# A fused attention and long-convolution kernel: the first quarter of x emptied in four chunks by two engines, the queries' bank emptied in one operation, the filter copies given other planned durations

## The chip, the cores and the metric

One core of a Trainium2 chip. It has a matrix engine (PE in the profile, its weight loads PEld), a vector engine (DVE), an activation engine (ACT), a general engine (POOL) and an engine that only issues transfers (SP). PE writes its results to eight banks of PSUM, each 128 partitions by 512 fp32 numbers; DVE and ACT empty them into SBUF. The metric is the device time of one execution in microseconds, median of several; lower is better.

## The reference

The kernel computes two things and puts them side by side: a multi-head attention block (2048 tokens, width 512, 32 heads of 16) and a long convolution with gates on the same shape. Cut to its core:

```python
def _A_ref(x, wqkv, wo):                      # x: 2048 x 512
    q, k, v = split_heads(x @ wqkv)           # 32 heads of 16
    scores = einsum("bhqd,bhkd->bhqk", q, k) * 16 ** -0.5
    p = softmax(scores)
    return merge_heads(einsum("bhqk,bhkd->bhqd", p, v)) @ wo

def _B_ref(q, k, v, shift_k, ssm_k, ssm_D):   # each of q, k, v: 2048 x 512
    kv = causal_conv4(k, shift_k) * v
    y = causal_long_conv(kv, ssm_k)           # 2048 taps per channel, by FFT
    return q * (y + kv * ssm_D)

out = concatenate([a, b], axis=-1)
```

## The kernel before

**Attention.** The scores are made in blocks of 128 keys by 512 queries for one head; there are 2048 such blocks (4 quarters of queries, 8 groups of 4 heads, 16 key tiles). Blocks are worked off in 695 steps, called T in the code, of two or three blocks each. In a step PE makes the blocks' scores (line L690) into two or three neighbouring PSUM banks, and ACT takes the exponential of the whole step in one ACTIVATE (L697) into the tile PT. In 260 of the steps the last block goes to DVE instead: L713 takes it out of its bank, and six short passes over pairs or fours of such blocks (L746 to L753) make the exponential there. PE then multiplies by the values (L787). The steps alternate between banks 0 to 2 and 3 to 5; bank 6 collects the products with the values, and bank 7, BGB in the code, serves everything else ("background").

**What is made ahead.** Queries QT, keys KTo and values VAF come out of projections of x (L396, L403, L441), each 128 x 512 in a bank that DVE empties (L419, L433, L452). The queries of a bank belong to two groups of heads; they are emptied twice, each time multiplied by another column of the mask MSK (evac_q, two TENSOR_SCALARs of 128 x 512). x arrives in quarters of 512 tokens. The last three are turned by the transfer itself; the first is turned on PE (turn_x, L375, 16 transposes), and its two halves are emptied by one ACTIVATE (L382) and one COPY (L384), 128 x 1024 each. The first query projection needs both halves.

**The convolution.** The taps are laid out for it by 16 filter copies, each of which is two COPYs of 128 x 1440 and 128 x 1380 (L502) and a short one (L508, from KZ0, which POOL makes out of the taps at L492 and L493). They are written to memory and come back in shifted pieces (WR). They read the taps that the transfers into QT, EI and JNK bring. The convolution itself is 8192 small matmuls (L944), whose moving operand is read in runs of 4 numbers.

**What sets the order.** The program is written by a planner in the file itself. It keeps a clock for each engine, adds an assumed duration for each operation, and decides step by step which piece of background, which pass on DVE and which filler goes where. The assumed durations set the order of instructions and nothing else. Each engine then works its list in order and waits on semaphores alone. On DVE the planner subtracts DVE_OVER (0.084 us) from what an operation is given. KZ_US is the assumed duration of half a filter copy; such a half is put in place when DVE's clock leaves room for it, and at the latest four steps after its turn. keep_share adds filler matmuls (L1114) where the planner finds PE too little used. At the start, `warm` runs 12 matmuls on zeros (L536). At the end, wait_busy runs filler matmuls (L1298) until the last transposed result of DVE (L828) is due, which the last output projection (L868) needs.

## Time and profile before

| | us |
|---|---|
| median of 3 runs | 833.1 (832.81 to 834.8) |
| the profiled execution, its own time | 833.18 |
| its span, first to last instruction | 831.4 |
| ACT busy | 813.6 (98%) |
| DVE busy | 788.7 (95%) |
| PE busy | 728.8 (88%) |

A group of instructions is read like this: line, engine, operation, what is written and read with its shape, how many, then busy time, mean duration of one in ns, and idle time of the engine just before them with the operation that ended it. The mean duration is longer than the distance from one instruction to the next where instructions of one engine overlap. In a timeline the columns are start, length, engine, line, and a count where neighbours are merged; in square brackets stands the idle time before and what ended it. The chain of waits goes back from the last instruction to whatever released it each time; its rows are start and length.

### The profile page before, as it was taken

The numbers are of one execution on the slowest core, as the hardware profiler recorded it, in microseconds if no ns is written. First come the engines' busy times: TensorE is split into PE (matmuls) and PEld (weight loads), VectorE is DVE, ScalarE is ACT, GpSimd is POOL, SyncE is SP. The second block draws the span as 40 slices with busy tenths as digits, with TensorE's granted clock in tenths as the row PEclk, the third lists the DMA queues.
The fourth block names the chain that finished last, engine by engine and source line by source line (L and its number), as shares of the span: only waits on it lengthen the run. The fifth ranks groups of instructions, "written<-read, shape, count | busy, mean of one in ns | idle before, by whom it ended". The sixth has DMA issues, their size and how long they took to land.

```text
span 831.4 us, 30085 instructions
## 1 busy us (share of the span) xinstructions
PE 728.8 (88%) x13456; PEld 322.7 (39%) x13456; DVE 788.7 (95%) x1423; ACT 813.6 (98%) x701; POOL 15.7 (2%) x35
## 2 busy tenths in 40 slices
PE   8888999988888889888889898988888888888997
PEld 3332334344434433334434444334443444434322
DVE  3799999999999999999999999999999999999995
ACT  6999999999999999999999999999999999999997
POOL 3000000000000001000000000000000000000000
PEclk9999999999999999999999999999999999999999
DMA  9977502058767776867775889567777988858200
GB/s 241 294 287 248 158 2 76 1 137 267 239 200 228 233 226 199 223 192 228 229 222 166 278 238 275 183 199 220 260 218 261 265 284 267 286 160 258 74 1 26
DMA packets 123856, 167.31 MB, mean 201 GB/s; under 512 B 50384, under 2 KB 55504, under 8 KB 123472
## 3 DMA queue, kind: packets, MB, share of 16 engines
q1 hardware_dynamic: 120752, 162.77, 63.1%
q8 instruction: 106, 1.74, 0.8%
q10 hardware_dynamic: 2400, 1.05, 0.6%
q0 software_dynamic: 576, 1.57, 0.5%
q14 instruction: 22, 0.18, 0.1%
HBM read 143.14 MB, written 16.52 MB: 192 GB/s over the span
## 4 chain that ended last, share of the span: by engine, by line
ACT 82%; DVE 10%; PE 4%; SPq 2%; DMA 1%; issue 1%; POOL 0%; DVEq 0%
ACT PT L697 82%; SPq L278 2%; DVE WR L502 1%; DVE EI L713 1%; PE PS L690 1%; DVE EI L753 1%; DMA JNK<-in_B_ssm_D_dram 1%; PE PS L787 1%; DVE EA L749 1%; DVE QT L419 1%; DVE KTo L433 1%; PE PS L465 1%; DVE EA L748 0%; DVE xT L746 0%; DVE EA L746 0%
## 5 line engine op out<-in xcount | busy, mean ns | idle before, releaser
L697 ACT ACTIVATE PT<-PS 128x1024 bf16<-128x1024 f32 (+1 forms) x695 | 809.7, 1417 | 5.5 <-PE PS L690 4.9
L690 PE MATMUL PS<-QT,KTo 32*128 32x512 bf16 x2048 | 272.5, 385 | 83.6 <-ACT PT L697 61.4
L787 PE MATMUL PS<-PT,VAF 128*32 128x512 bf16 x1788 | 226.3, 391 | 0.9
L944 PE MATMUL PS<-WR,KV 128*8 128x64 bf16 (+15 forms) x8192 | 183.6, 214 | 2.5 <-issue 2.0
L713 DVE TENSOR_SCALAR EI<-PS 128x512 int32<-128x512 f32 x260 | 173.9, 682 | 1.5 <-PE PS L690 1.1
L944 PEld LDWEIGHTS PS<-WR,KV 128*18 128x18 bf16 (+15 forms) x8192 | 150.1, 119 | 47.4 <-issue 24.2
L690 PEld LDWEIGHTS PS<-QT,KTo 32*128 32x128 bf16 x2048 | 70.9, 91 | 235.3 <-ACT PT L697 213.0
L753 DVE SCALAR_TENSOR_TENSOR EI<-EI,EA 128x1024 int32<-128x1024 int32 (+1 forms) x146 | 156.5, 1098 | 0.0
L787 PEld LDWEIGHTS PS<-PT,VAF 128*32 128x32 bf16 x1788 | 53.6, 93 | 92.2 <-issue 86.6
L1114 PE MATMUL PS<-ZR,IDN 128*128 128x512 bf16 (+3 forms) x299 | 84.0, 333 | 0.0
L749 DVE TENSOR_TENSOR EA<-EA,xT 128x1024 f16<-128x1024 f16 x114 | 75.2, 683 | 0.0
L746 DVE TENSOR_SCALAR xT<-EI 128x1024 f16<-128x1024 uint16 x114 | 74.0, 684 | 1.3
L752 DVE TENSOR_TENSOR EA<-EA,xT 128x1024 bf16<-128x1024 f16 x114 | 75.0, 682 | 0.0
L787 PE MATMUL PS<-EI,VAF 128*32 128x512 bf16 x260 | 56.3, 410 | 1.3 <-DVE STG L835 0.6
L750 DVE TENSOR_SCALAR xT<-xT 128x1024 f16<-128x1024 f16 x114 | 45.1, 418 | 0.0
L748 DVE TENSOR_SCALAR EA<-xT 128x1024 f16<-128x1024 f16 x114 | 44.0, 420 | 0.0
L1114 PEld LDWEIGHTS PS<-ZR,IDN 128*128 128x128 bf16 x299 | 23.2, 97 | 32.3 <-issue 23.0
L787 PEld LDWEIGHTS PS<-EI,VAF 128*32 128x32 bf16 x260 | 13.1, 93 | 32.6 <-issue 14.2
L835 DVE STREAM_TRANSPOSE STG<-PS 128x512 f32<-128x512 f32 x31 | 22.0, 711 | 3.4 <-PE PS L787 3.3
L419 DVE TENSOR_SCALAR QT<-PS,MSK 128x512 bf16<-128x512 f32 x32 | 22.6, 741 | 1.2 <-PE PS L396 1.2
L403 PE MATMUL PS<-xT,WKV 128*128 128x512 bf16 x60 | 19.4, 386 | 3.8 <-DVE VAF L452 1.3
L396 PE MATMUL PS<-xT,WQ 128*128 128x512 bf16 x64 | 20.1, 385 | 2.1 <-ACT xT L382 0.8
(72 smaller groups left out, 317.2 us busy)
## 6 DMA issues: line engine op xcount, KB each, us to landing
WR<-kz_scratch SPq DMA_DIRECT2D x512, 256.0 KB, 4.0
kz_scratch<-WR SPq DMA_DIRECT2D x16, 752.0 KB, 4.4
QN<-in_B_q_dram SPq DMA_DIRECT2D x16, 128.0 KB, 4.2
out_dram<-KV SPq DMA_DIRECT2D x16, 128.0 KB, 4.1
out_dram<-OUTA POOLq DMA_DIRECT2D x12, 128.0 KB, 2.9
QT<-in_B_ssm_k_dram SPq DMA_DIRECT2D x1, 1024.0 KB, 5.6
EI<-in_B_ssm_k_dram SPq DMA_DIRECT2D x1, 1024.0 KB, 8.4
STG<-in_B_v_dram SPq DMA_DIRECT2D x1, 1024.0 KB, 7.4
```

What stands on the lines that cost most here:

```text
L690: ins = e.matmul(PS[:, bank, :], lhsT=KTo[32 * s:32 * s + 32, g // 2, kt * 128:(kt + 1) * 128], rhs=QT[32 * s:32 * s + 32, qb % 2, g, :], ...
L697: h_exp[T] = act.op(lambda e: e.activation(PT[:, T % R_PT, 0:n * QB], PS[:, banks[0]:banks[0] + n, :].rearrange("p b f -> p (b f)"), ACT.E ...
L713: s.fix.append(dve.op(lambda e: e.tensor_scalar(EI[:, i, :], PS[:, bank, :], FIX_LO, FIX_ADD, ALU.max, ALU.add), [h] + old + [x for o in s ...
L746: step(2, lambda sl: lambda e: e.tensor_scalar(eb[:, sl], frac[:, sl], FS / OCT, -FS * ROOT0, ALU.mult, ALU.add), s.fix + old)
L748: step(4, lambda sl: lambda e: e.tensor_scalar(ea[:, sl], eb[:, sl], FS * (ROOT0 - ROOT1), None, ALU.add))
L749: step(2, lambda sl: lambda e: e.tensor_tensor(ea[:, sl], ea[:, sl], eb[:, sl], ALU.mult))
L750: step(4, lambda sl: lambda e: e.tensor_scalar(eb[:, sl], eb[:, sl], C1 * BITS / FS ** 3, (C0 + C1 * ROOT0) * BITS / FS ** 2, ALU.mult, AL ...
L752: step(2, lambda sl: lambda e: e.tensor_tensor(eg[:, sl], ea[:, sl], eb[:, sl], ALU.mult))
L753: step(1, lambda sl: lambda e: e.scalar_tensor_tensor(ei[:, sl], ei[:, sl], BITS / OCT, eg[:, sl], ALU.mult, ALU.add), ends=True)
L787: ins = e.matmul(PS[32 * s:32 * s + 32, pvb(qb * NG + g), :], lhsT=VAF[:, kt, h * VW:h * VW + 32], rhs=rhs, start=(order[b] == 0), stop=(o ...
L944: ins = e.matmul(PS[32 * c:32 * c + NW - 2 * n, BGB, col:col + 64], lhsT=KV[:, 2 * n:NW, 4 * qd + c], rhs=w, start=(n == 0), stop=(n == NB ...
L1114: return e.matmul(PS[:, bank, col:col + 128 * k], lhsT=IDN[:, :], rhs=ZR[:, :].rearrange("p (m d) -> p m d", m=1).broadcast_to([128, 4 * k ...
```

## The change

Four things change. The first quarter of x is turned in four groups of four transposes, each into a bank of its own, and emptied by four operations of 128 x 512, two on DVE and two on ACT in turn; the first query projection is issued in four pieces, each of which waits for its own chunk alone; 10 matmuls stand in `warm` where 12 stood, on bank 4. The queries' bank is emptied by one TENSOR_TENSOR that writes both groups (128 x 1024 out of 128 x 512 read twice, times the mask's two columns spread out); only the very first one, for group 0 of quarter 0, keeps the old pair. The planner is told 0.57 us and 0.19 us for the parts of a filter copy in place of 0.5 and 0.22. And before the last filler of the end, 32 small matmuls of VAF with itself are put in, in four kinds that differ in how the moving operand is read (runs of 4, of 2, of 1, and one whole run of 64 numbers). Nobody reads what they write.

```diff
-KZ_US = .5
+KZ_US = .57
...
-    def turn_x(sc, cp, bank, eng):
-        pbf = PS[:, bank, :].bitcast(BF16)
+    def turn_x(sc, c, bank, eng):
+        pbf = PS[:, bank, 0:256].bitcast(BF16)
...
-            for i in range(2):
-                for t in range(4):
-                    c = 2 * cp + i
-                    ins = e.transpose(pbf[:, 512 * i + 128 * t:512 * i + 128 * t + 128],
-                                      KVE[:, 4 * sc + t, 128 * c:128 * c + 128], IDN[:, :])
+            for t in range(4):
+                ins = e.transpose(pbf[:, 128 * t:128 * t + 128], KVE[:, 4 * sc + t, 128 * c:128 * c + 128], IDN[:, :])
...
-            deps += h_x[qb] + [h_wq[min(o, 1)]]
+            deps += (x or h_x[qb]) + [h_wq[min(o, 1)]]
...
+    def evac_both(qb, o, bank, h):
...
+        src = PS[:, bank, :].rearrange("p (m f) -> p m f", m=1).broadcast_to([128, 2, QB])
+        par = MSK[:, :].rearrange("p (m f) -> p m f", f=1).broadcast_to([128, 2, QB])
+        bank_free[bank] = h_q[(qb, 2 * o)] = h_q[(qb, 2 * o + 1)] = dve.op(
+            lambda e: e.tensor_tensor(QT[:, qb % 2, 2 * o:2 * o + 2, :], src, par, ALU.mult), [h, h_msk], us=1.24)
...
-        h_kzp[i] = dve.op(lambda e: e.tensor_copy(KZS[:, i % 4, :, 0, :], k0), [h_kzt[0], h_kz0] + hs, us=0.22)
+        h_kzp[i] = dve.op(lambda e: e.tensor_copy(KZS[:, i % 4, :, 0, :], k0), [h_kzt[0], h_kz0] + hs, us=0.19)
...
-    pe.op(lambda e: warm(e, 12, 0), [h_w0], us=3.5)
-    turn_x(0, 0, 0, act)
-    turn_x(0, 1, 1, dve)
-    hq = pe_unit(("q", 0, 0), 6)
+    pe.op(lambda e: warm(e, 10, 4), [h_w0], us=3.0)
+    for c in range(4):
+        turn_x(0, c, c, act if c % 2 else dve)
+    hq = None
+    for c in range(4):
+        hq = pe_unit(("q", 0, 0), 6, [c], [h_xc[c]])
...
+    def wait_busy0(bank):
...
+        def runs_of_1(e):
+            return [e.matmul(PS[32 * c:32 * c + 32, bank, 0:64], lhsT=VAF[:, n, 32 * c:32 * c + 32], rhs=va(n, [[68, 64]]),
+                             start=True, stop=True, tile_position=(0, 32 * c)) for n in range(2) for c in range(4)][-1]
...
+        for fn in (runs_of_4, runs_of_2, runs_of_1, whole_runs):
+            pe.op(fn, [h_idn, bank_free[bank]], us=0.16)
...
     for t in range(4):
+        if t == 0:
+            wait_busy0(0)
         wait_busy(when_of(h_otn[(NQB * NO - 1, 2 * (t // 2) + 2)]), 0)
```

The planner makes a new order out of this, on DVE from the passes over the first pair of blocks on. The numbers of instructions stay where they were: 695 exponentials on ACT (398 of three blocks, 297 of two), 260 blocks on DVE, 32 filter-copy halves; the fillers on L1114 go from 299 to 296. Lines after the new functions are 6 higher (L690 becomes L696, L697 L703, L713 L719, L433 L437, L868 L874).

DVE in the opening, from the seventh emptied block of keys (KTo) to the eighth, before:

```order
L433 CAST KTo<-PS 128x512
L835 STREAM_TRANSPOSE STG<-PS 128x512
L502 COPY WR<-EI 128x24x60
L813 RECIPROCAL DR<-STG 128x32
L817 TENSOR_TENSOR OB<-STG,DR 128x2x16x16
L477 TENSOR_TENSOR KV<-PS,STG 128x4x128
L502 COPY WR<-EI 128x23x60
L508 COPY WR<-KZ 128x47x4
L502 COPY WR<-EI 128x24x60
L828 STREAM_TRANSPOSE OT<-OB 128x512
L433 CAST KTo<-PS 128x512
```

The same stretch in the changed program:

```order
L437 CAST KTo<-PS 128x512
L841 STREAM_TRANSPOSE STG<-PS 128x512
L506 COPY WR<-EI 128x24x60
L819 RECIPROCAL DR<-STG 128x32
L481 TENSOR_TENSOR KV<-PS,STG 128x4x128
L506 COPY WR<-EI 128x23x60
L512 COPY WR<-KZ 128x47x4
L823 TENSOR_TENSOR OB<-STG,DR 128x2x16x16
L719 TENSOR_SCALAR EI<-PS 128x512
L506 COPY WR<-EI 128x24x60
L437 CAST KTo<-PS 128x512
```

The transpose of OB has moved behind the block of keys, and a block of scores (L719) is taken from its bank ahead of it; a second L719 has moved ahead of the seventh block in the same way. From the start to the eighth block of keys DVE's list now holds two more L719, one transpose less, and one L423 in place of one pair of L419.

PE at the end of the program, before (L787 is the last product with the values, L1298 the fillers, L868 the last output projections):

```order
L787 MATMUL PS<-PT,VAF 32x512 x2
L868 MATMUL PS<-WKV,OT 128x512
L868 MATMUL PS<-WKV,STG 128x512
L1298 MATMUL PS<-IDN 128x512 x3
L868 MATMUL PS<-WKV,STG 128x512 x2
```

And now:

```order
L793 MATMUL PS<-PT,VAF 32x512 x2
L874 MATMUL PS<-WKV,OT 128x512
L874 MATMUL PS<-WKV,STG 128x512
L1310 MATMUL PS<-VAF 32x64 x8
L1314 MATMUL PS<-VAF 32x64 x8
L1318 MATMUL PS<-VAF 32x64 x8
L1322 MATMUL PS<-VAF 32x64 x8
L1298 MATMUL PS<-IDN 128x512
L874 MATMUL PS<-WKV,STG 128x512 x2
```

Two of the three fillers have given way to the 32 small matmuls.

38 lines of the change are left out of this document (23 added, 15 removed).

## The prediction

> **What bounds the kernel now.** I read the page's first part and its costliest groups first, then the table by stages, to see which engine has no room left and where.
>
> ```profile
> PE 728.8 (88%) x13456; PEld 322.7 (39%) x13456; DVE 788.7 (95%) x1423; ACT 813.6 (98%) x701; POOL 15.7 (2%) x35
> ...
> L697 ACT ACTIVATE PT<-PS 128x1024 bf16<-128x1024 f32 (+1 forms) x695 | 809.7, 1417 | 5.5 <-PE PS L690 4.9
> ...
> 25.00:100.00 75.00, 65.00 (x546) 24.50 (x543) 71.40 (x164) 71.79 (x64) 0.39 (x4) 1.00 0.81 262
> ...
> 600.00:700.00 100.00, 86.66 (x2099) 42.03 (x2096) 97.16 (x161) 98.90 (x86) 1.08 (x2) 0.98 0.83 261
> ```
>
> In the stage rows the busy times are those of PE, PEld, DVE, ACT and POOL. ACT is the bound: even in the latest of the stages shown it is idle 1.1 us in 100, where DVE has 2.8, and 809.7 of its 813.6 us are the exponentials. The order of the changed program still holds 398 + 297 of them in the same two shapes, so these 809.7 us stay. What can move is what lies around them, which ACT's timeline shows (start, length, then the idle time before):
>
> ```profile
> 9.80 18.44 ACT L697 ACTIVATE PT<-PS 128x1536 bf16<-128x1536 f32 x16 [0.75 <-PE PS L690]
> ...
> 28.63 10.77 ACT L697 ACTIVATE PT<-PS 128x1024 bf16<-128x1024 f32 x10 [0.39 <-PE PS L690]
> ...
> 73.88 36.97 ACT L697 ACTIVATE PT<-PS 128x1024 bf16<-128x1024 f32 x31 [0.75 <-PE PS L690]
> ...
> 454.81 198.32 ACT L697 ACTIVATE PT<-PS 128x1536 bf16<-128x1536 f32 x169 [0.39 <-PE PS L690]
> 653.89 1.46 ACT L697 ACTIVATE PT<-PS 128x1536 bf16<-128x1536 f32 x1 [0.76 <-PE PS L690]
> 655.68 168.59 ACT L697 ACTIVATE PT<-PS 128x1536 bf16<-128x1536 f32 x146 [0.33 <-PE PS L690]
> ```
>
> The first exponential starts at 9.80, the last ends at 655.68 + 168.59 = 824.27. Check: 9.80 + 809.7 + (5.5 - 0.75) idle = 824.25. The end takes 831.4 - 824.27 = 7.1 us, and 833.18 - 831.4 = 1.8 us lie outside the span. After 100 us the idle time is 0.39 + 0.76 + 0.33 = 1.5 us; so 5.5 - 0.75 - 1.5 = 3.25 us lie between 28 and 100 us, where DVE is busy 71.40 of 75. Everything that the change can win is in four places: 9.80 at the start, 3.25 in the opening, 1.5 later, 7.1 at the end.
>
> **The start.** PE turns the quarter at 5.61; both halves must be out before the queries' matmuls start.
>
> ```profile
> 5.61 1.06 PE L375 MATMUL PS<-IDN,KV 128*128 128x128 bf16 x16
> ...
> 6.25 1.02 ACT L382 ACTIVATE xT<-PS 128x1024 bf16<-128x1024 bf16 x1 [1.42 <-PE PS L375]
> ...
> 7.50 1.02 PE L396 MATMUL PS<-xT,WQ 128*128 128x512 bf16 x4 [0.83 <-ACT xT L382]
> ...
> L884 ACT ACTIVATE QT<-PS 128x512 bf16<-128x512 f32 x2 | 1.2, 597 | 3.2 <-PE PS L868 3.2
> ```
>
> In chunks, ACT takes its first at 6.25 as now (eight transposes are done then) for 0.60, its second from 6.85 to 7.45 at the latest, or 0.25 us earlier if two ACTIVATEs overlap as the exponentials do (mean 1417 ns, 809.7/695 = 1165 ns apart). Three of the four matmuls are over by then; the last comes 0.23 us after its chunk, as now (7.27 to 7.50), and takes 0.39, as the single L868 at 826.31 does further down. The queries are ready at 7.8 to 8.07 in place of 8.52, so the first exponential starts 0.45 to 0.7 us earlier. The two matmuls fewer in `warm` fall into PE's wait for x, which ends with x's landing and not with them. But the gain is met again at 28 us. The chain of waits of the first 100 us runs there:
>
> ```profile
> 15.38 8.21 DMA JNK<-in_B_ssm_D_dram
> ...
> 25.60 0.61 DVE VAF L452
> ...
> 28.30 0.69 DVE KTo L433
> ```
>
> The taps land at 23.6 by SP's own sequence, which the change does not touch. DVE's first filter copy waits for them, the values' bank (L452) is queued behind it, PE's next projection behind that, and the keys come out at 28.30; the exponential of 28.63 waits for these. DVE's list is the same up to there in both programs. So ACT arrives 0.45 to 0.7 earlier and waits that much longer: I count **0**, with bounds -0.7 (all kept) and 0 (what is done earlier makes nothing later).
>
> **The opening, 28 to 100 us.** From 28.30 on the chain lies almost wholly on DVE.
>
> ```profile
> 30.91 0.60 DVE EI L713
> ...
> 76.37 0.62 DVE OT L828
> 76.99 0.57 DVE KTo L433
> ...
> 80.81 1.32 DVE QT L419 x2
> ...
> 192.11 2.28 DVE EI L753 x2
> ```
>
> Up to the eighth block of keys (76.99 here) the new list holds two more L713 (+2 x 0.60), a transpose less (-0.62), and one wide operation for a pair. The wide operation is in no trace. Bounds of its distance: 1.14, as 128 x 1024 of L753 (2.28 for two), and 1.32 as the pair; the nearest rows are products out of PSUM and with a spread fp32 operand:
>
> ```profile
> L974 DVE TENSOR_TENSOR KV<-PS,QN 128x512 bf16<-128x512 f32 x16 | 10.9, 680 | 0.6 <-PE PS L964 0.6
> ...
> L817 DVE TENSOR_TENSOR OB<-STG,DR 128x512 bf16<-128x512 f32 x15 | 10.4, 690 | 0.4
> ...
> L753 DVE SCALAR_TENSOR_TENSOR EI<-EI,EA 128x1024 int32<-128x1024 int32 x114 | 135.3, 1215 | 0.0
> ...
> L753 DVE SCALAR_TENSOR_TENSOR EI<-EI,EA 128x512 int32<-128x512 int32 x32 | 21.2, 681 | 0.0
> ```
>
> At 128 x 512 they last as long as L753 (680, 690, 681 ns), so I take L753's 1.14: -0.18. Sum on DVE: 1.20 - 0.62 - 0.18 = +0.4. Behind the two L713 are then the next keys, queries and PE's score matmuls that need them. Since ACT has two blocks less by then and catches them up later (1592 - 1182 = 410 ns each by the two exponential rows below), the worst is 0.4 + 0.82 = +1.2.
>
> ```profile
> L697 ACT ACTIVATE PT<-PS 128x1536 bf16<-128x1536 f32 x398 | 559.8, 1592 | 2.8 <-PE PS L690 2.5
> L697 ACT ACTIVATE PT<-PS 128x1024 bf16<-128x1024 f32 x297 | 301.9, 1182 | 2.8 <-PE PS L690 2.4
> ...
> 34.73 1.34 DVE L502 COPY WR<-QT 128x1440 bf16<-128x1440 bf16 x2
> 35.99 0.24 DVE L508 COPY WR<-KZ 128x188 bf16<-128x188 bf16 x1
> ```
>
> Against this stands the planner's better knowledge. Half a filter copy really takes (35.99 - 34.73)/2 = 0.63; the planner counted 0.5 - 0.084 = 0.42 and now counts 0.49: a third of the miss (0.07 of 0.21) is gone, and urgent banks are less often queued behind a copy thought shorter. If a third of the 3.25 us idle goes with it, that is -1.1. Bounds of the whole stage: -3.25 and +1.2; I take +0.4 - 1.1 = **-0.7**.
>
> **After 100 us.** Twelve of the fifteen wide operations stand here, 12 x 0.18 = 2.2 us less on DVE. ACT is busy 98.90 of 100 us there by the stage's row, which hides it: 0. Without that cover it would be up to -2.2, but the exponentials alone then set the pace, and there is nothing below them. The 1.5 us idle are the clock's:
>
> ```profile
> 448.61:452.02 3.41, 2.40 (x65) 1.29 (x56) 3.41 (x8) 3.41 (x4) 0.00 (x0) 1.00 0.88 280
> 452.02:455.43 3.41, 3.40 (x45) 0.99 (x47) 3.41 (x5) 3.02 (x4) 0.00 (x0) 0.50 0.53 173
> ...
> 650.00:653.41 3.41, 1.42 (x48) 0.77 (x35) 2.72 (x4) 3.13 (x3) 0.00 (x0) 1.00 0.58 124
> 653.41:656.82 3.41, 3.41 (x64) 1.36 (x61) 2.87 (x6) 2.60 (x2) 0.00 (x0) 0.50 0.92 254
> ...
> 652.88 0.49 PE L944 MATMUL PS<-WR,KV 128*30 128x64 bf16 x23 [1.67 <-issue]
> ```
>
> Behind a stretch with PE busy 2.40 or 1.42 of 3.41 us follows one with the granted clock at 0.50, and ACT waits in it. The second begins with 1.67 us in which PE waited for nothing shown. The Trainium skill ("TensorE: Matmul & The Clock Gate", Part 1: The HAM clock gate) has the clock fall after an idle window of about 3.4 us; the trace disagrees, since PE was busy 2.40 of 3.41 us before the first fall. By that rule a new order could not bring such a stretch, by the rows it can. Bounds: -1.5 (none) to +3.0 (three times as much); with 296 fillers for 299 I take **0**.
>
> **The end.** The last output projection waits for DVE (L828) until 826.31.
>
> ```profile
> 825.10 0.81 PE L1298 MATMUL PS<-IDN 128*128 128x512 bf16 x3
> ...
> 826.31 0.39 PE L868 MATMUL PS<-WKV,STG 128*128 128x512 bf16 x1 [0.41 <-DVE STG L828]
> ...
> 649.50 0.68 PE L944 MATMUL PS<-WR,KV 128*14 128x64 bf16 x32
> ```
>
> The 32 new matmuls have the convolution's size, 32 of which take 0.68; with one filler (0.27, a third of 0.81) they end by 825.10 + 0.95 = 826.05, before 826.31. Cost **0**; if each took twice as long, 826.73, so +0.4; with the 0.21 us of a full 512-column step for each group of four, 8 x 0.21 + 0.27 = 1.95, so +0.75 at the most. The Trainium skill ("SBUF — State Buffer", Door 1: The DMA port swizzle) says that reading slows when fewer than two numbers of a 16-byte line are used in turn, which would hit the runs of one; no row here shows it, and it stays inside these bounds.
>
> **Sum.** 833.18 + 0 - 0.7 + 0 + 0 = **832.5 us**, made against the profiled execution, which stands 0.1 us above the median of 833.1. 0.3% of it, 2.5 us, is about what a measurement of this kernel can tell from no change.
>
> **The rivals.** Faster: the opening is really opened. The start's 0.6 is kept, since the new order feeds ACT other work at 28 us, and two thirds of the 3.25 us go without the +0.4: 833.18 - 0.6 - 2.2 - half of the clock's 1.5 = 829.6. For it: DVE's own idle time there is 75 - 71.40 = 3.6 us, so DVE is not full. Against it: the landing at 23.6.
>
> Slower, by the clock: a new order, planned with the same miss about PE, leaves PE too little used in more stretches. One fall cost 0.39 us of idle time, the other 0.76 + 0.33 = 1.1; three more of the dearer kind make 833.18 + 3.3 = 836.5, and the time is slower by over 0.3% from the third on. For it: before one of the falls PE was busy 70%, not far below its 87% of a whole stage. Against it: only two falls in 212 stretches of 3.41 us between 100 and 824 us so far.
>
> Slower, by the wide operation: if DVE does not take a bank read twice at the pace of L974, and needs twice the 1.14, twelve times 1.14 = 13.7 us come on a DVE that has 2.84 idle in 100, and each holds up whatever L713 is queued behind it, whose bank PE's next scores need; if two thirds reach ACT, 833.18 + 9 = 842. Against it speak the rows of L974 and L817.
>
> Without effect on the sign: the two early L713 cost their full 1.2 and the end 0.4, so 833.18 + 1.6 = 834.8, within 0.3%.
>
> **How the numbers follow.** Chances: the forecast 0.42, the faster rival 0.27, the clock 0.16, the wide operation 0.05, early L713 and end 0.05, and 0.05 for a new order that is slower in a way I don't see. Faster by over 0.3% is then 0.27, within 0.3% 0.47, slower 0.26. The forecast's own range is 830.8 to 834.6. For 8 in 10 the range must take in the faster rival (829.6, with a little below it for a start that is kept in full) and most of the clock's (836.5): 829.0 to 836.2.
>
> **What would show it.** ACT's first exponential near 9.2 and a longer wait before the exponential at about 28.6: the start is won and given back. Idle time of ACT between 28 and 100 us near 2.5 (without the start's): the opening as I have it. L423 near 1215 ns: the wide operation. Stretches with the clock at 0.50 between 100 and 820 us: two, as now; four or more and the clock's rival is right. The last 7.1 us unchanged: the small matmuls are hidden. I am wrong if the exponential of 28.6 starts at 28.0, or if ACT's idle time after 100 us has grown beyond 3 us.

## The result, and the profile after

| | before | changed |
|---|---|---|
| median of 6 runs each, same chip (us) | 833.24 (832.49 to 834.8) | 843.81 (839.82 to 849.87) |
| ratio of the times | 1 | 1.0128, 95% interval 1.0107 to 1.0149 |
| profiled execution: its own time, span | 833.18, 831.4 | 842.49, 840.7 |
| first exponential starts, last 7.1 us begin | 9.80, 824.3 | 8.99, 833.6 |
| ACT busy with exponentials, idle before them | 809.7, 5.5 | 811.0, 14.3 |

The changed kernel is slower by 1.3%, outside the range that was given. The page's first part and the group of the exponentials, in the changed kernel:

```profile
PE 727.3 (87%) x13443; PEld 322.8 (38%) x13481; DVE 788.2 (94%) x1409; ACT 815.0 (97%) x702; POOL 17.5 (2%) x35
...
L703 ACT ACTIVATE PT<-PS 128x1536 bf16<-128x1536 f32 (+1 forms) x695 | 811.0, 1387 | 14.3 <-PE PS L696 13.9
```

The work is the same; ACT waits longer for it. Of the 9.3 us of span, -0.8 lie at the start, +1.3 in the exponentials' own time (they overlap their neighbours a little less), +8.8 in idle time before them, and nothing at the end. The table by stages, with the busy times of PE, PEld, DVE, ACT and POOL, then the granted clock, shows both places that the prediction spoke of:

```profile
25.00:100.00 75.00, 63.18 (x524) 23.44 (x531) 68.79 (x158) 67.51 (x61) 1.02 (x4) 0.95 0.83 263
600.00:700.00 100.00, 85.59 (x2119) 43.02 (x2119) 94.09 (x156) 97.48 (x84) 0.54 (x1) 0.97 0.82 259
```

ACT has lost 4.3 us in the opening (71.79 busy before) and 1.4 in the later stage (98.90), and DVE is less busy in both (71.40 and 97.16 before): no engine is short of time. ACT's timeline says where it stood, in brackets (two of its windows, up to 100 us and from 650):

```profile
8.99 17.27 ACT L703 ACTIVATE PT<-PS 128x1536 bf16<-128x1536 f32 x15 [0.75 <-PE PS L696]
28.05 1.02 ACT L703 ACTIVATE PT<-PS 128x1024 bf16<-128x1024 f32 x1 [1.79 <-PE PS L696]
30.54 1.94 ACT L703 ACTIVATE PT<-PS 128x1024 bf16<-128x1024 f32 x2 [1.47 <-PE PS L696]
33.25 12.08 ACT L703 ACTIVATE PT<-PS 128x1024 bf16<-128x1024 f32 x11 [0.77 <-PE PS L696]
...
60.17 1.94 ACT L703 ACTIVATE PT<-PS 128x1024 bf16<-128x1024 f32 x2 [0.58 <-PE PS L696]
63.18 8.24 ACT L703 ACTIVATE PT<-PS 128x1536 bf16<-128x1536 f32 x7 [1.07 <-PE PS L696]
...
662.35 4.14 ACT L703 ACTIVATE PT<-PS 128x1536 bf16<-128x1536 f32 x3 [1.55 <-PE PS L696]
666.85 1.45 ACT L703 ACTIVATE PT<-PS 128x1536 bf16<-128x1536 f32 x1 [0.36 <-PE PS L696]
668.91 43.00 ACT L703 ACTIVATE PT<-PS 128x1024 bf16<-128x1024 f32 x37 [0.61 <-PE PS L696]
712.63 1.45 ACT L703 ACTIVATE PT<-PS 128x1536 bf16<-128x1536 f32 x1 [0.72 <-PE PS L696]
```

Each wait ends with PE's scores, so the next question is what PE waited for. DVE's timeline holds the two places of the opening:

```profile
23.80 1.18 DVE L506 COPY WR<-QT 128x1440 bf16<-128x1440 bf16 x2 [2.54 <-DMA JNK<-in_B_ssm_D_dram]
...
25.70 0.68 DVE L456 CAST VAF<-PS 128x512 bf16<-128x512 f32 x1
...
29.99 0.69 DVE L437 CAST KTo<-PS 128x512 bf16<-128x512 f32 x1 [2.98 <-PE PS L400]
...
51.03 1.23 DVE L423 TENSOR_TENSOR QT<-PS,MSK 128x1024 bf16<-128x1024 f32 x1
52.16 0.72 DVE L506 COPY WR<-QT 128x1380 bf16<-128x1380 bf16 x1
52.79 0.25 DVE L512 COPY WR<-KZ 128x188 bf16<-128x188 bf16 x1
...
61.23 0.69 DVE L481 TENSOR_TENSOR KV<-PS,QT 128x512 bf16<-128x512 f32 x1 [1.84 <-DMA QT<-in_B_v_dram]
```

First, the taps: the copy at 23.80 holds the values' bank (L456) behind it, and PE's next projection of keys waits for that bank. The bank itself is only 0.18 us later than before (25.70 for 25.52), but PE, whose earlier work is done sooner, stands still for 2.38 us in place of 0.98. PE's timeline, first of the kernel before, then of the changed one, and the windows of the changed one:

```profile
26.25 0.60 PE L403 MATMUL PS<-xT,WKV 128*128 128x512 bf16 x2 [0.98 <-DVE VAF L452]
```

```profile
26.84 0.63 PE L400 MATMUL PS<-xT,WKV 128*128 128x512 bf16 x1 [2.38 <-DVE VAF L456]
```

```profile
22.69:26.10 3.41, 1.77 (x17) 0.78 (x13) 1.74 (x4) 3.41 (x3) 1.58 (x3) 0.99 0.94 188
26.10:29.51 3.41, 2.67 (x12) 0.50 (x13) 0.91 (x2) 1.18 (x2) 0.00 (x0) 0.50 1.03 246
```

The clock is at 0.50 from 26.1 us on, and the keys come out at 29.99 instead of 28.30; the run below with this wait filled shows that the clock makes them late. Second, the end of the eighth filter copy gives free the buffer into which the second half of v is loaded. It ends with the L512 at 52.79, before with this line:

```profile
49.12 0.24 DVE L508 COPY WR<-KZ 128x188 bf16<-128x188 bf16 x1
```

About 1.7 of these 3.7 us are the late keys; besides, the wide emptying of the queries' bank (L423) now stands ahead of the copy. The chain of waits (start, length) runs through that load of v, and later through a tap load that PE waits for:

```profile
53.43 7.71 DMA QT<-in_B_v_dram
...
655.95 5.27 DMA WR<-kz_scratch
```

DVE waits 1.84 us for v, which it did not before. PE's timeline has the later waits:

```profile
159.74 0.39 PE L696 MATMUL PS<-QT,KTo 32*128 32x512 bf16 x3 [1.41 <-DVE QT L423]
...
661.26 0.50 PE L950 MATMUL PS<-WR,KV 128*32 128x64 bf16 x20 [1.83 <-DMA WR<-kz_scratch]
...
711.51 0.33 PE L950 MATMUL PS<-WR,KV 128*20 128x64 bf16 x13 [1.43 <-issue]
```

At 159.74 the scores wait for the wide operation itself; at 661 for a tap load; at 711 for nothing that the trace names. The clock falls to 0.50 for nine stretches of 3.41 us between 26 and 716 us (at 26.1, 381.0 and 660.9 for two each, at 408.4, 456.1 and 712.1 for one), where the kernel before had two. One such pair by windows:

```profile
708.73:712.14 3.41, 1.67 (x51) 0.87 (x43) 3.38 (x5) 3.18 (x3) 0.00 (x0) 1.00 1.00 309
712.14:715.56 3.42, 3.42 (x44) 1.06 (x41) 1.25 (x4) 2.60 (x2) 0.00 (x0) 0.50 1.00 344
```

PE was busy 1.67 of 3.41 us ahead of the fall. Behind it PE is busy all the time, with fewer matmuls (44 after 51): each takes longer at half the clock, and now ACT waits (2.60 busy of 3.42). The twenty traces of this document show 73 such falls ahead of the end of the kernel. Each comes behind a stretch of 3.41 us in which PE was busy 2.45 us or less; but not each such stretch has a fall behind it (in the changed kernel, PE was busy 1.87 us from 60.20 to 63.61, and the clock stayed), so the traces give no sharp border.

### The profile page after: what moved, and what is told of

Same layout as the page of the kernel before. It is cut to its first block, busy times and chain, and to the rows that moved or that the text cites. A ratio compares the mean times of both kernels' runs of the same rounds, so it can differ in the third digit from the quotient of the medians.

```text
span 840.7 us, 30100 instructions
## 1 busy us (share of the span) xinstructions
PE 727.3 (87%) x13443; PEld 322.8 (38%) x13481; DVE 788.2 (94%) x1409; ACT 815.0 (97%) x702; POOL 17.5 (2%) x35
## 4 chain that ended last, share of the span: by engine, by line
ACT 76%; DVE 12%; PE 5%; DMA 3%; SPq 2%; issue 1%; POOL 0%; DVEq 0%
ACT PT L703 76%; SPq L278 2%; PE PS L696 2%; DVE EI L719 2%; DVE WR L506 1%; DVE EI L759 1%; PE PS L793 1%; DMA WR<-kz_scratch 1%; DVE EA L755 1%; DMA JNK<-in_B_ssm_D_dram 1%; DMA QT<-in_B_v_dram 1%; DVE EA L752 1%; DVE EA L754 1%; DVE EA L758 1%; PE PS L950 1%
## 5 line engine op out<-in xcount | busy, mean ns | idle before, releaser
L703 ACT ACTIVATE PT<-PS 128x1536 bf16<-128x1536 f32 (+1 forms) x695 | 811.0, 1387 | 14.3 <-PE PS L696 13.9
L696 PE MATMUL PS<-QT,KTo 32*128 32x512 bf16 x2048 | 276.5, 389 | 89.7 <-ACT PT L703 64.9
L950 PE MATMUL PS<-WR,KV 128*16 128x64 bf16 (+15 forms) x8192 | 184.1, 214 | 5.0 <-DMA WR<-kz_scratch 2.9
L719 DVE TENSOR_SCALAR EI<-PS 128x512 int32<-128x512 f32 x260 | 173.4, 684 | 2.5 <-PE PS L696 2.0
L950 PEld LDWEIGHTS PS<-WR,KV 128*16 128x16 bf16 (+15 forms) x8192 | 149.5, 120 | 51.1 <-issue 26.4
L696 PEld LDWEIGHTS PS<-QT,KTo 32*128 32x128 bf16 x2048 | 70.9, 91 | 237.5 <-ACT PT L703 206.5
L1114 PE MATMUL PS<-ZR,IDN 128*128 128x512 bf16 (+3 forms) x296 | 82.0, 331 | 0.0
L1114 PEld LDWEIGHTS PS<-ZR,IDN 128*128 128x128 bf16 x296 | 23.3, 97 | 34.4 <-issue 24.2
L963 DVE CAST YB<-PS 128x256 bf16<-128x256 f32 (+1 forms) x37 | 14.1, 381 | 10.5 <-PE PS L950 9.9
L400 PE MATMUL PS<-xT,WKV 128*128 128x512 bf16 x47 | 16.7, 400 | 6.1 <-DVE VAF L456 2.4
L278 POOL DMA_DIRECT2D out_dram<-OUTA x12 | 8.3, 688 | 652.2 <-DVE OUTA L881 652.2
```

Of the source, the lines that this page charges most:

```text
L696: ins = e.matmul(PS[:, bank, :], lhsT=KTo[32 * s:32 * s + 32, g // 2, kt * 128:(kt + 1) * 128], rhs=QT[32 * s:32 * s + 32, qb % 2, g, :], ...
L703: h_exp[T] = act.op(lambda e: e.activation(PT[:, T % R_PT, 0:n * QB], PS[:, banks[0]:banks[0] + n, :].rearrange("p b f -> p (b f)"), ACT.E ...
L719: s.fix.append(dve.op(lambda e: e.tensor_scalar(EI[:, i, :], PS[:, bank, :], FIX_LO, FIX_ADD, ALU.max, ALU.add), [h] + old + [x for o in s ...
L950: ins = e.matmul(PS[32 * c:32 * c + NW - 2 * n, BGB, col:col + 64], lhsT=KV[:, 2 * n:NW, 4 * qd + c], rhs=w, start=(n == 0), stop=(n == NB ...
L1114: return e.matmul(PS[:, bank, col:col + 128 * k], lhsT=IDN[:, :], rhs=ZR[:, :].rearrange("p (m d) -> p m d", m=1).broadcast_to([128, 4 * k ...
```

## The experiments

All runs below were timed against the kernel before on the same chip; it stood at 832.7 to 834.1 in these comparisons. A difference between two changed kernels is one of medians out of separate comparisons, each with an interval of about 0.2% either way, so that 1 or 2 us of it show little without the traces. Two things were asked. Which part of the change costs the 10 us? And is it a place, a stall with its price, or the order of work as such?

**The parts, one at a time.** The new start on the order of before (the planner's clocks were set back to their old values, rounded here, behind the start, so that every engine's list is the old one from there):

```diff
+    pe.op(lambda e: warm(e, 10, 4), [h_w0], us=3.0)
+    for c in range(4):
+        turn_x(0, c, c, act if c % 2 else dve)
...
+    pe.t, act.t, dve.t = 7.957, 8.567, 8.979
```

> The kernel before with the new start alone (chunks, 10 warm matmuls); everything behind the start stands in the order of the kernel before. Theory A (an earlier start makes PE's wait for the taps at 24 to 26 us longer, the clock falls to 0.50 there and ACT loses more than the start won): first exponential near 9.0, granted clock 0.50 in a stretch near 26 us, ACT idle between 27 and 35 us 2 us or more above the kernel before, time 834.5 to 837. Rival B (the loss comes from the new order alone): first exponential near 9.0, the clock stays, time 832.4 to 833.3.

Measured: 833.83, ratio 1.0005 (0.9988 to 1.0023). ACT's timeline:

```profile
9.06 17.27 ACT L701 ACTIVATE PT<-PS 128x1536 bf16<-128x1536 f32 x15 [0.75 <-PE PS L694]
27.34 1.02 ACT L701 ACTIVATE PT<-PS 128x1024 bf16<-128x1024 f32 x1 [1.01 <-PE PS L694]
28.75 10.76 ACT L701 ACTIVATE PT<-PS 128x1024 bf16<-128x1024 f32 x10 [0.39 <-PE PS L694]
```

The start wins 0.74 us and ACT waits 1.0 us longer at 27 to 29 us: the ten exponentials that started at 28.63 start at 28.75. On the old order the start is worth nothing and costs nothing, within the interval of 0.2%. PE waits 1.84 us for the values' bank in this trace and the clock does not fall, against theory A; the trace doesn't show why it stayed. Its mirror image, the changed kernel's order with the old start:

```diff
-    pe.op(lambda e: warm(e, 10, 4), [h_w0], us=3.0)
+    pe.op(lambda e: warm(e, 12, 0), [h_w0], us=3.5)
+    turn_x(0, 0, 0, act)
+    turn_x(0, 1, 1, dve)
...
+    pe.t, act.t, dve.t = 7.076, 7.686, 8.098
```

> The changed kernel with the old start (two halves, 12 warm matmuls); everything behind the start stands in the order of the changed kernel. Theory A: no fall of the clock near 26 us, ACT idle between 27 and 35 us like the kernel before (about 0.8 us), time 2.5 to 4 us below the changed kernel, 839.5 to 841. Rival B: time within 1 us of the changed kernel.

Measured: 842.84, ratio 1.011 (1.0092 to 1.0129). So 8.7 of the 10.6 us come with the order, as rival B said. Then the wide operation and the planner's two costs, each alone, each with the order that the planner makes of it:

```diff
-                    (us, first), (0.0, lambda: evac_q(u[1], u[2], 1, bank, h[0]))]
+                    (us, lambda: evac_both(u[1], u[2], bank, pe_unit(u, bank, range(4 - UNIT, 4))))]
```

> The kernel before with the queries' bank emptied in one operation and nothing else of the change; the order is planned anew from there. Theory R (any new order costs several us, because the stalls of PE for instruction fetches and tap loads fall elsewhere after 640 us and the clock falls behind them; before's order is a good one of many): 835 to 843, as the order of the other threshold (839.7). Besides, the wide operation itself: PE waits for it at step 124 (near 157 us), 1.41 us, ACT idle 0.39. Theory W (the wide operation is what costs, in whatever order): as the changed kernel, 842 or more, and the costs alone (the next run) give 833 to 834. Rival K (the filter copies' costs are what spoils the order): 833 to 834.5 here, 842 or more in the next run.

```diff
-KZ_US = .5
+KZ_US = .57
...
-        h_kzp[i] = dve.op(lambda e: e.tensor_copy(KZS[:, i % 4, :, 0, :], k0), [h_kzt[0], h_kz0] + hs, us=0.22)
+        h_kzp[i] = dve.op(lambda e: e.tensor_copy(KZS[:, i % 4, :, 0, :], k0), [h_kzt[0], h_kz0] + hs, us=0.19)
```

> The kernel before with the planner's costs of the filter copies (0.57 and 0.19) and nothing else of the change; planned anew. Theory R: 835 to 843. Theory W: 833 to 834. Rival K: 842 or more. In none of them the wait of 1.41 us at step 124.

Measured: the wide operation alone 834.37 (1.0004, 0.9987 to 1.0021), the costs alone 834.71 (1.0009, 0.9993 to 1.0025). Theory W and rival K fall, and theory R in its sharp form too: these new orders cost 0.8 and 1.2 us by the medians, and some 2 at the most by the intervals. With the wide operation alone PE doesn't wait for it at step 124 either, so that wait belongs to the order as well. DVE's timeline near 50 us shows why neither part does the harm that both do together. The wide operation alone, then the costs alone:

```profile
49.65 0.25 DVE L515 COPY WR<-KZ 128x188 bf16<-128x188 bf16 x1
...
50.34 1.24 DVE L426 TENSOR_TENSOR QT<-PS,MSK 128x1024 bf16<-128x1024 f32 x1
```

```profile
48.49 0.76 DVE L419 TENSOR_SCALAR QT<-PS,MSK 128x512 bf16<-128x512 f32 x1
...
49.78 0.26 DVE L508 COPY WR<-KZ 128x188 bf16<-128x188 bf16 x1
49.94 0.76 DVE L419 TENSOR_SCALAR QT<-PS,MSK 128x512 bf16<-128x512 f32 x1
```

With the wide operation alone the filter copy still comes ahead of it. With the higher cost alone the copy comes later, but slips between the two halves. Only with both does it stand behind all 1.2 us.

**Another order without any change.** One threshold of the planner (when DVE's fillers go ahead of a wait) at 0.51 instead of 0.5:

```diff
-FILL_LATE = 0.5
+FILL_LATE = 0.51
```

> The kernel before with one of the planner's thresholds moved by a hundredth of a microsecond (FILL_LATE 0.5 to 0.51) and nothing else: the same instructions in another order. Theory C (the order of the kernel before is a lucky one; any other order costs several us after 100 us): time 836 or more, three or more falls of the clock after 100 us. Rival (orders are alike, the loss belongs to the change): 832 to 834.5.

Measured: 839.66, ratio 1.0065 (1.0039 to 1.0091). A new order can cost 5 us with no part of the change in it. Its seven runs lie between 833.37 and 841.1, at mean granted clocks of 0.996 to 0.980; the profiled one is the 833.37, with two stretches at 0.50, so theory C's three falls are in no trace, and only the times and clocks of the other runs speak for them.

**The named places, cured one at a time in the changed kernel.** The wait for the taps is filled with nine matmuls that add zeros:

```diff
+            if T == 14:
+                pe.ops.append(([], lambda e: [e.matmul(PS[:, PVB, :], lhsT=IDN[:, :], rhs=ZR[:, :].rearrange("p (m d) -> p m d", m=1).broadcast_to([128, 16, 32]), start=False, stop=False) for _ in range(9)][-1], None))
```

> The changed kernel, order and start kept, with 9 filler matmuls (they add zeros to a bank in use) where PE waits for the taps at 24 us. If the clock is what costs there, it stays at 1.00 between 22 and 33 us and ACT's idle time between 27 and 35 us falls from 4.0 us to 1.8 or less; time 2 to 3 us below the changed kernel. If the late keys alone cost it, the idle time stays above 3 us.

Measured: 842.68 (1.0098, 1.0076 to 1.0119), 1.1 us less than the changed kernel, where 2 to 3 were expected. In its trace the clock stays up until 158 us, and ACT's waits at 27 to 29 us are those of the new start alone (1.04 and 0.39). The two operations of the eighth filter copy put ahead of the seven before them in DVE's list (the expectation counts six), with the waits renumbered; the cut has the numbers put in:

```diff
+    dve.ops[61:70] = dve.ops[68:70] + dve.ops[61:68]
```

> The changed kernel with the two operations of its eighth filter copy put ahead of the six DVE operations before them (of the DVE exponential, and the wide emptying of the queries' bank), so that the second half of v is loaded from 50.6 instead of 53.0 us. Nothing else moves. Theory L: DVE's wait of 1.84 us at 61.2 goes, and with it ACT's idle 0.58 at 60.2 and 1.07 at 63.2: 843.8 - 1.6 = 842.2 (841 to 843.3); the excess of the stage up to 104 us falls from 6.1 to about 4.5. Rival (the six operations that come 0.9 us later are what the next exponential waits for): DVE is late by 0.9 instead, no gain, 843.8.

Measured: 841.6 (1.0101, 1.008 to 1.0123), where 842.2 was expected. DVE's timeline has no wait for v any more:

```profile
58.92 0.69 DVE L481 TENSOR_TENSOR KV<-PS,QT 128x512 bf16<-128x512 f32 x1 [0.51 <-PE PS L469]
```

and from the start of step 18 to that of step 80 ACT takes 72.21 us instead of 73.57 (73.46 in the kernel before). Then SP's queue: three groups of tap loads that the planner held back until PE's next instruction fetch, and no load held at all.

```diff
-            h_wr[qd] = dma(sp, d_wr[r], WR[r][:, c, :], src, [h_kzs[i] for i in range(12, 16)] + [h] + hold, takes=SET_US)
+            h_wr[qd] = dma(sp, d_wr[r], WR[r][:, c, :], src, [h_kzs[i] for i in range(12, 16)] + [h] + hold, takes=SET_US,
+                           free=hold if qd in (99, 111, 125) else (), quad=qd)
```

(What stands in `free` counts for the planner's clock and is not waited for.)

> The changed kernel with its order on PE, ACT and DVE, and one thing different on SP: the tap loads of the three groups 99, 111 and 125 wait only for the buffer that they fill, not for the planner's instruction fetch as well, and those of group 99 go ahead of the four loads of q and the store. In the traces of the changed kernel, of the old start with the new order and of the filled tap wait, these loads start 4.8 to 6.1 us after their buffer came free, and PE waits for them at 661, 708 to 712 and 769 us. Theory L (late supplies: the loss of the new order sits in a few named waits, each with a clock fall behind it): ACT's idle places at 662 to 669 (1.55+0.36+0.61), 712 to 717 (0.72+0.34+0.21) and 773 to 777 (0.48+0.34) go, 4.6 us: 843.8 - 4.6 = 839.2 (838 to 840.5), granted clock 0.988 or more. Rival F (the loads were held for a reason: unheld they delay an instruction fetch, and PE starves at the same places): 842 to 845, with waits of PE put down to issue at 655, 703 and 764. Rival S (a slower order loses in whatever place: waits turn up elsewhere): 842 to 844, with no wait at the three places.

```diff
-                           free=hold if qd in (99, 111, 125) else (), quad=qd)
+                           free=hold, quad=qd)
```

> The changed kernel with the same order on every engine and on SP's queue, but none of the 76 tap loads that the planner holds back for an instruction fetch waits for it; each waits for its buffer alone. Theory L: 111 and 125 are early again, 99 still stands behind the loads of q: 843.8 - 2.1 = 841.7 (840 to 843). Rival F: loads go ahead of instruction fetches in 76 places; if one in five of them starves PE by 1.5 us, and costs 1.1 us of clock besides, 843.8 + 15 x 2.6 = over 860, and any time above 846 with more waits of PE put down to issue speaks for it.

Measured: 843.91 (1.0133, 1.011 to 1.0156) and 843.75 (1.0109, 1.0079 to 1.0138): no gain in either. With the three early, PE's timeline has the wait for a tap load 15 us later and a stall put down to issue at 709 still:

```profile
676.17 0.38 PE L953 MATMUL PS<-WR,KV 128*32 128x64 bf16 x12 [1.36 <-DMA WR<-kz_scratch]
...
708.76 0.62 PE L795 MATMUL PS<-PT,VAF 128*32 128x512 bf16 x4 [1.36 <-issue]
```

Theory L was wrong for the last stage: a stall cured there comes up at another place. That holding loads matters as much as rival F says is refuted too, since 76 loads let go cost nothing. The remedies together, then with the queries' bank in two operations again:

> The changed kernel with the three remedies together: nine matmuls that add zeros in the wait for the taps at 24 to 27 us, the second half of v loaded earlier, and the tap loads of groups 99, 111 and 125 early. Theory L: the losses add up, 843.8 - 1.1 - 1.6 - 4.6 = 836.5 (835 to 838.5), clock 0.992 or more: most of the 10.6 us is then placed. Rival S: each place that is cured lets another come up, 840 or more.

```diff
-            lambda e: e.tensor_tensor(QT[:, qb % 2, 2 * o:2 * o + 2, :], src, par, ALU.mult), [h, h_msk], us=1.24)
+        for par in range(2):
+            h_q[(qb, 2 * o + par)] = dve.op(
+                lambda e, par=par: e.tensor_scalar(QT[:, qb % 2, 2 * o + par, :], PS[:, bank, :], MSK[:, par:par + 1], None, ALU.mult),
+                [h, h_msk], us=0.662)
```

> The kernel with all four places cured, and the queries' bank emptied in two operations again, one behind the other in the place of the wide one in the same order of every engine. Theory (the wide operation makes PE wait at step 124 by holding its first half back until the whole is done): PE's wait of 1.41 us there falls to about 0.8, ACT's 0.39 goes, and the clock falls at 157 to 164 us that came behind it in three of six profiles of the new order go too: 837.6 - 0.4 - about 1.1 = 836.1 (834.8 to 837.3). Rival (the two operations take 0.1 us more in 16 places and delay the DVE exponentials behind them): 837.6 to 839.

Measured: 837.56 (1.0058, 1.0036 to 1.0079) and 840.04 (1.0073, 1.0047 to 1.01). The first is 6.3 us of the 10.6 less, where theory L said 7.3; one at a time the three remedies gave 3.2 by the medians, and the record doesn't show where the rest comes from. The narrow operations did not help, against both forecasts: PE's wait at step 124 fell from 1.41 to 0.94 us, ACT's idle 0.39 stayed.

**The last stage, and the whole.** Open was whether the rest belongs to the order after 640 us, so that was made anew, in three ways, and once with the opening cured as well.

```diff
-LAG_US = 0.068
+LAG_US = 0.0682
```

> The changed kernel with the planner's cost of one conv step at 0.0682 instead of 0.068 us; the order on PE is the changed kernel's up to 645 us (but for some rows at 295 us) and another after it. Theory N: the excess of the last stage (from 624 us) falls from 8.7 to 3 to 5 us, 844 - 4.5 = 839.5 (837.5 to 841.5). Rival M: 843 to 845, excess 8 to 10 again.

```diff
-FILL_LATE = 0.5
+FILL_LATE = 0.51
```

> The changed kernel with one threshold of the planner at 0.51 instead of 0.50 (the one that decides when DVE's fillers go ahead of a wait); the order on PE is the changed kernel's up to 300 us, and another after it. Theory N (the loss after 300 us belongs to the one order that the changed kernel drew, by the places where its stalls after 640 us fall): another draw, 836 to 842, nearer 839.5 if its last stage has an excess of 3 to 5 us instead of 8.7. Rival M (the change itself makes every order of its kind slow): 843 to 845.

```diff
-    pe.op(lambda e: warm(e, 10, 4), [h_w0], us=3.0)
+    pe.op(lambda e: warm(e, 12, 0), [h_w0], us=3.5)
+    turn_x(0, 0, 0, act)
+    turn_x(0, 1, 1, dve)
```

> The wide operation and the copy costs with the old start; its order on PE is the changed kernel's up to 706 us, with other rows after it. It keeps the places at 53 us (second half of v), 157 us (the wide operation) and 655 to 664 us (tap load of group 99). Theory N: as the old start with the new order, 842.8, less what the rows after 706 us save there, 1 to 3: 840 to 842. Rival (the combination of the parts needs the new start to lose): 833 to 835.

```diff
-LAG_US = 0.068
+LAG_US = 0.0682
...
+    dve.ops[14:18] = [dve.ops[17]] + dve.ops[14:17]
+    dve.ops[61:70] = dve.ops[68:70] + dve.ops[61:68]
```

> The kernel whose last stage is ordered anew, with the values' bank emptied ahead of the first filter copy (as in the run of that name on the old order, which won 2.4 us there) and the eighth filter copy ahead of the wide operation (which won 2.2 us on the changed kernel). Theory N: 839.5 - 2.4 - 2.0 = 835 (833 to 837). Rival M: 839 or more.

Measured: 843.3 (1.0122, 1.0101 to 1.0143), 838.93 (1.0049, 1.0026 to 1.0071), 842.92 (1.0109, 1.0086 to 1.0132) and 835.1 (1.0018, 1.0006 to 1.0029). The last stage alone is not the cause: made anew it saved 0.5 us, as rival M said; in the profiled run PE stalled near 772 us in place of 661 and 711. The third has the old start, so its measure is the changed order with the old start, 842.84: new rows after 706 us saved nothing, and the two parts lose with the old start too. Made anew from 300 us it saved 4.9, so no order of the later stages is fixed by the change, and rival M falls there. With the opening cured on top of the first of them, 8.2 went. In the two profiles 5.3 of them went between the first exponential and step 80 (92.7 us instead of 98.0). Its 835.1 is what theory N forecast, but not by its sum: the opening gave what the last stage was to give.

**The clock by itself.** In that last kernel the wait for the wide operation at step 124 was filled with six matmuls that add zeros. The wait stays, only the clock can gain.

```diff
+    pe.ops.insert(at_, ([], lambda e: [e.matmul(PS[:, PVB, :], lhsT=IDN[:, :], rhs=ZR[:, :].rearrange("p (m d) -> p m d", m=1).broadcast_to([128, 16, 32]), start=False, stop=False) for _ in range(6)][-1], None))
```

> The kernel of the run before (last stage ordered anew, two places cured) with six matmuls that add zeros in PE's wait of 1.41 us for the wide operation at step 124. The wait for the wide operation stays. Theory (the clock falls because PE stands still there, and that costs about 1.1 us for each stretch of 3.4 us): no fall between 150 and 170 us, ACT's idle 0.39 stays, the 0.60 + 0.60 + 0.20 behind it go: 835.1 - 1.4 = 833.7 (832.7 to 834.7). Rival (the stall alone counts, or the filling delays the scores): 835 or more.

Measured: 832.61, ratio 0.9995 (0.9983 to 1.0008): 2.5 us less by the medians, 1.9 by the ratios, and the time of the kernel before. ACT's timeline and the windows (PE's busy time first, the clock third from the end) without the filling:

```profile
155.25 4.15 ACT L703 ACTIVATE PT<-PS 128x1024 bf16<-128x1024 f32 x4 [0.39 <-PE PS L696]
160.00 1.45 ACT L703 ACTIVATE PT<-PS 128x1536 bf16<-128x1536 f32 x1 [0.60 <-PE PS L696]
162.06 1.45 ACT L703 ACTIVATE PT<-PS 128x1536 bf16<-128x1536 f32 x1 [0.60 <-PE PS L696]
```

```profile
152.76:156.18 3.42, 2.01 (x18) 0.60 (x18) 3.42 (x9) 3.03 (x4) 0.00 (x0) 1.00 0.00 0
156.18:159.59 3.41, 3.41 (x18) 0.66 (x16) 3.17 (x6) 3.05 (x4) 0.00 (x0) 0.50 0.00 0
```

and with it:

```profile
155.77 19.53 ACT L703 ACTIVATE PT<-PS 128x1024 bf16<-128x1024 f32 x17 [0.39 <-PE PS L696]
```

```profile
153.41:156.83 3.42, 3.31 (x24) 1.12 (x21) 3.42 (x9) 3.03 (x4) 0.00 (x0) 1.00 0.00 0
```

The stall costs 0.39 either way. The fall behind it cost 0.60 and 0.60 and some more in that trace, and was avoided by work that computes nothing. The fall doesn't come every time: of the eleven traces with the wait of 1.41 us unfilled, seven show it.

**A version that beats both.** The new start on the old order, with the emptying of the values' bank moved ahead of the first filter copy on DVE:

```diff
+    dve.ops[14:18] = [dve.ops[17]] + dve.ops[14:17]
```

> The run with the new start and the old order, with one operation of DVE put elsewhere: the emptying of the values' bank goes ahead of the first filter copy, which waits for the taps until 23.7 us, instead of behind it. Theory (the start is given back only because this copy holds DVE's queue): the emptying starts near 24.2 instead of 25.6, the keys' matmuls at 24.8 instead of 26.4, the exponential of 28.6 comes 0.7 to 1.4 us earlier: 833.8 - 0.7 to 1.4 = 832.4 to 833.1, and faster than before by a tenth of a per cent, if the later waits don't take it. Rival (the next copies and keys are late by the same 0.6 us, or the taps' filters hold the end): 833.8 or more.

Measured: 831.48, ratio 0.9979 (0.9963 to 0.9995). ACT's first wait after its start is now at 38.62, and the one at 28 us is gone:

```profile
9.23 29.08 ACT L701 ACTIVATE PT<-PS 128x1536 bf16<-128x1536 f32 x26 [0.75 <-PE PS L694]
38.62 3.43 ACT L701 ACTIVATE PT<-PS 128x1536 bf16<-128x1536 f32 x3 [0.31 <-PE PS L694]
```

DVE empties the bank at 24.42 instead of 25.63, and the keys follow. It won more than the 0.7 to 1.4 us that were expected. The same with a wait at 50 us filled too:

```diff
+    pe.ops.insert(at_, ([], lambda e: [e.matmul(PS[:, PVB, :], lhsT=IDN[:, :], rhs=ZR[:, :].rearrange("p (m d) -> p m d", m=1).broadcast_to([128, 16, 32]), start=False, stop=False) for _ in range(3)][-1], None))
```

> The quickest kernel so far (old order, new start, values' bank first) with three matmuls that add zeros in PE's wait of 0.72 us at 49.6 us, ahead of a product's matmuls. Theory: the fall of 3.4 us at 50.3 goes, ACT's idle at 52.7 falls from 1.36 to about 0.3 as in the kernel before: 831.5 - 0.5 to 1.0 = 830.5 to 831.0, where runs had that fall. Rival (the fall comes in few runs, or the filling delays the product): 831.5 or more.

Measured: 831.64, ratio 0.9982 (0.9969 to 0.9995), so no further gain over the one before, as the rival said. In its trace the fall at 50.3 us is gone and others stand at 226.7 and 452.0.

## Why the prediction was wrong, step by step

**The start** (0, between -0.7 and 0) is the first step that failed, by its bound "what is done earlier makes nothing later". Its size was near: it said 9.1 to 9.35 for the first exponential, which starts at 8.99. On the old order it was worth 0, as counted. In the new order PE's longer stand ahead of the late bank is followed by a fall of the clock at 26 to 28 us, in all six traces that have the new start and the new order without a cure there, and in neither of the two with the old start. So the gain is not only given back: step 18 starts at 33.25 where it started at 30.46. With the wait filled it starts at 30.57, which shows that the clock makes this delay. In the medians the old start (1.0 us less) and the filling (1.1 less) are worth little more than the noise. That one filter copy holds the values' bank behind it on DVE is shown by moving that bank ahead: there the gain is kept, and 2.0 us in all are won over the kernel before.

**The opening, 28 to 100 us** (-0.7) is the second, by its term "against this stands the planner's better knowledge", -1.1. From the first exponential to step 80 the changed kernel took 97.8 us, the kernel before 94.1: +3.7. Of this +3.6 lies ahead of step 18, 0.8 as the start's gain given back and 2.8 behind the fall just told. From step 18 to step 80 it is 73.57 for 73.46, so nothing was won there either. The higher costs moved the eighth filter copy later while the wide operation became one piece, and the second half of v, which hangs on that copy through SP, came 1.84 us late. The prediction named the taps as a landing that sets the pace and never asked what else hangs on a filter copy, though a load was queued behind the eighth. In the four traces of kernels with this copy put earlier and the wide operation kept, the same 62 steps take 72.2 to 72.7 us, 0.7 to 1.3 less than before: about the gain that was forecast was there, and the load of v took it. Putting this copy earlier alone gave 2.2 us back in the medians.

**The wide operation** was sized right. Fifteen of them take 1218 ns each in the groups by shape, and 1.13 us apart in the chain. What was missed is not its length but that nothing of it is ready before all is: at step 124 PE waits 1.41 us. In two halves it still waited 0.94, so most of that wait is that the queries' matmuls are issued only just before they are needed: in the kernel with the last stage made anew and two places cured the last of them (L393) ends at 153.40, L423 starts at 153.44, and PE has nothing else to do until it ends.

**After 100 us** (0, between -1.5 and +3.0) is the third, and most of the loss lay there: from step 80 to the end it is 733.9 us in place of 727.5, +6.4, outside the bounds. The premise that failed is "with 296 fillers for 299 I take 0". The number of fillers says nothing of where PE stalls; the planner puts fillers only where its own clock sees room, and a stall that it does not see gets none. The clock rival had the mechanism. Three more falls after 100 us did come (five for two), but two of the five lasted two stretches each, another of two came at 26 us, and the stalls ahead of the falls cost something besides; so its 836.5 was too low by 7 us. By the prediction's own signs, four or more stretches after 100 us (there are seven) and idle time beyond 3 us there (5.85), it was this rival that was right.

**The end** was right: the last 7.1 us are unchanged, and the 32 small matmuls are hidden.

**How much is the clock.** Over 253 timed runs of the twenty kernels, time goes with the mean granted clock at 604 us for the whole of it (correlation 0.92), that is 1.2 us for each stretch of 3.41 us at half, 0.00205 of a run. The changed kernel's mean is 0.981, before's 0.997: 9.8 of the 10.5 us between the means. But this line puts the stalls of an order into the price of its falls, as both come together. Taken within each kernel, every run against its own kernel's mean, the slope is 430 us (correlation 0.83): 0.9 us for a stretch, and 7.0 of the 10.5. So the clock is an estimated two thirds or more of the loss. That a fall costs time of its own, without the stall ahead of it, is shown by the filled waits, for two places.

The Trainium skill ("TensorE: Matmul & The Clock Gate", Part 1: The HAM clock gate) has the clock fall after an idle window of about 3.4 us. The traces disagree on the threshold, with falls behind 2.01 and 1.67 us of PE busy in 3.4, and agree on the 3.4 us: each fall lasts 3.41 us or a multiple.

What is left open: the stalls put down to issue. The long ones take 1.0 to 2.5 us each and come at other places in each order; the planner takes them for instruction fetches, and no run here settles it. The changed kernel's own last stage was not run with the three cures that bring the time of the kernel before (the values' bank first, the eighth copy early, the wait at step 124 filled), so its share beside them is not known. Why the new start brings the fall at 26 us with the new order, and did not in the one trace with the old order, is open too.

## What to carry to other kernels

Where a planner's costs set the order, correcting a cost is a change of the whole order, and its effect is not the cost's size: two parts that each gave an order as good as the old one gave together one that was 9 to 10 us worse, and a threshold moved by 0.01 cost 5. So look in the new order, queue by queue, for what hangs on each operation that moved, loads on another engine's queue above all, and count where the engine behind the bound stands still long enough for its clock to fall. A stall that can't be removed can be filled: six matmuls on zeros were worth about 2 us.

## What the hardware did that was not expected

The four kinds of small matmuls at the end, eight each, in the changed kernel's PE timeline:

```profile
834.51 0.27 PE L1310 MATMUL PS<-VAF 128*32 128x64 bf16 x8
834.59 0.31 PE L1314 MATMUL PS<-VAF 128*32 128x64 bf16 x8
834.71 0.44 PE L1318 MATMUL PS<-VAF 128*32 128x64 bf16 x8
834.96 0.25 PE L1322 MATMUL PS<-VAF 128*32 128x64 bf16 x8
```

By their starts, eight whose moving operand is read in runs of 4 take 0.08 us, in runs of 2 take 0.12, in runs of 1 take 0.25: short runs have a price in these rows, three times for runs of 1 and one and a half times for runs of 2, and the times are the same to 0.01 us in three other profiles. It was hidden here. The second thing is that the kernel's order, and not its work, carries so much: PE's busy time differs by 1.5 us between the two kernels, and their times by 10.
